# Three heads' columns of a weight block, loaded two rows to a partition by loads of eight partitions

## The chip, the cores and the metric

The kernel runs on one core of a Trainium2 chip. The metric is the device time of one execution in microseconds (us). The core has a matrix engine (TensorE, PE in the profile; its weight loads are PEld), a vector engine (VectorE, DVE), a scalar engine (ScalarE, ACT), GpSimd (POOL) and SyncE (SP), which here only issues transfers (DMAs). The transfers run on 16 DMA engines. On-chip memory (SBUF) has 128 partitions; matmuls write to banks of PSUM, each 128 partitions by 512 float32.

## The reference

A decode step of one transformer block: two batch rows of one token, D = 512, 32 query heads of 128, 8 key/value heads, a window of the last 4096 cached positions, a feed-forward layer of 1792. All is float32.

```python
mod = (silu(c) @ w_mod).reshape(2, 6, 1, -1)          # sa, ca, ga, sb, cb, gb
h = layernorm(x) * (1 + ca) + sa
q = h @ wq                                            # wq: 512 x 4096
# k, v: the last 4096 of 32768 positions, 8 heads, each used by 4 query heads
o = softmax(q k^T * 128**-0.5) v
x = x + ga * (o @ wo)                                 # wo: 4096 x 512
h = layernorm(x) * (1 + cb) + sb
x = x + gb * (silu(h @ w1) @ w2)                      # w1: 512 x 1792, w2: 1792 x 512
```

Keys and values are 64 MiB of the 97.5 MB that are read; the weights are the rest. Every weight, key and value is read once.

## The kernel before

**The stream.** All large operands pass through one ring of eight buffers of [128, 4096] float32 (`stream`, L69, `RING = 8`). A buffer can be filled again when everything that read it is done, so the transfer into the n-th buffer taken waits for the last reader of the (n-8)-th. All transfers are issued by SP, one after the other, in this order: `wm0` (the first 128 rows of `w_mod`, L103), four small ones for `c` and `x` (`c_ch`, `x_ch`, L107: four partitions each), `wm1` to `wm3` (L111), `wq0` to `wq3` (L112), then `fetch(0)` and `fetch(h + 1)` in the head loop: two tiles of keys (L79) and, from the second head on, two of values (L86) for each key/value head; at the end four tiles of `wo` (L473), a small one for `x` again (`x_sp`, L474), three of `w1` and five of `w2` (L95). The transfers' completions are counted on eight semaphores, taken in turn, so a ninth transfer isn't issued before the first of its eight has landed.

**The start.** `c` is put through silu and multiplied with `w_mod` in four steps of 128 rows (L241 to L255); layernorm of `x` runs beside it. The modulated row is transposed to `hq_T` (L263): [128, 4, 32], where `hq_T[p, k, :]` belongs to row 128*k + p of `wq`; of its 32 columns two hold the batch rows.

**The query projection** (L280 to L291). For each of the four row blocks k and each half n of the heads, four matmuls, one for each g = 0 to 3, write to partitions 32g to 32g+31 of the PSUM bank `q_ps[n]`. Head number 16n + 4s + g has its 128 columns at place s of that row group, so one matmul covers four heads, s = 0 to 3, 512 columns. The 16 matmuls of a row block wait for its tile of `wq`. Behind it (L292 to L311) q is transposed and spread into `qbd`, which the first scores need.

**The head loop** (L447 to L467). For each of the eight key/value heads VectorE transposes the keys (L337, eight instructions a head), TensorE forms scores (L349), and softmax, the turned probabilities and the product with the values (L423) follow one head later. In the loop the program's order is kept on each engine (`inorder`).

**The end.** `o @ wo` (L548 to L567), the second layernorm, `w1` (L593), silu, `w2` (L628 to L651; the last tile holds one row of `w2` a partition, 2 KB), the last two VectorE instructions (L653, L654) and the transfer of the output (L656). `busy` puts matmuls without use between (`junk`).

Of the kernel before, what the change touches and what calls it, by code (L numbers as in the profile page):

```python
# [13 lines left out]
P = 128  # L14
B, D = 2, 512
HQ, HKV, DH = 32, 8, 128
# [7 lines left out]
def adaln_block(  # L24
# [21 lines left out]
    nc = tc.nc  # L46
# [16 lines left out]
    def const(shape, name):  # L63
        return consts.tile(shape, F32, name=name)

    def bank(tag, name):
        return (psum1 if tag in "CO" else psum).tile([P, 512], F32, tag=tag, name=name)

    def stream(name):  # L69
        return ring.tile([P, 4096], F32, tag="st", name=name)  # L70

    def load_rows(name, w, k, width):
        t = stream(f"{name}{k}")[:, :width]
        nc.sync.dma_start(t, w[k * P : (k + 1) * P, :])
        return t
# [33 lines left out]
                src[b, :].rearrange("(k a c) -> a k c", k=4, a=4),  # L109
            )  # L110
    wm += [load_rows("wm", w_mod, k, 6 * D) for k in range(1, 4)]  # L111
    wqt = [load_rows("wq", wq, k, HQ * DH) for k in range(4)]  # L112


    ident = const([P, P], "ident")
# [125 lines left out]
    for k in range(4):  # L241
        ab = wm[k][:, : 2 * D].rearrange("p (s k a c) -> p a s k c", s=2, k=4, a=4)
        cd = wm[k][:, 2 * D :].rearrange("p (s g m) -> p g s m", s=4, g=4)
        for g in range(4):
            r = slice(32 * g, 32 * g + 32)
            nc.tensor.matmul(m_ch[r, :], scT[:, k, :], ab[:, g], start=(k == 0), stop=(k == 3))
        for g in range(4):
            r = slice(32 * g, 32 * g + 32)
# [13 lines left out]
    hq_T = const([P, 4, 32], "hq_T")  # L262
# [13 lines left out]
    nc.gpsimd.memset(uT, 0.0)  # L276

    q_ps = [bank("D", f"q{n}") for n in range(2)]  # L280
    for k in range(4):
        wv = wqt[k].rearrange("p (n s g m) -> p n g s m", n=2, s=4, g=G)
        for n in range(2):
            for g in range(G):
                nc.tensor.matmul(  # L285
                    q_ps[n][32 * g : 32 * g + 32, :],
                    hq_T[:, k, :],
                    wv[:, n, g],
                    start=(k == 0),
                    stop=(k == 3),  # L290
                )  # L291
    for n in range(2):  # L292
        qT = once.tile([P, D], F32, tag="wide", name=f"qT{n}").rearrange("p (s j r) -> p s j r", s=4, r=32)
        nc.vector.transpose(qT.rearrange("p s j r -> p (s j r)"), q_ps[n])  # L294
        for g in range(G):
            r = slice(32 * g, 32 * g + 32)
            eng = nc.gpsimd if g % 2 else nc.vector
            eng.tensor_copy(
                qg[n][r, :, :, :, g], qT[r, :, :, 0:32:16].rearrange("p s j b -> p s b j")
            )  # L300
        rp = bank("C", f"qr{n}")[:, :P]
        nc.tensor.matmul(
            rp, rep4, qg[n].rearrange("p s b j g -> p (s b j g)"), start=True, stop=True
        )
        for i in range(4):
            r = slice(32 * i, 32 * i + 32)
            cp = nc.scalar.copy if i % 2 else nc.vector.tensor_copy
            cp(
                qbd[n][r].rearrange("p s b j c -> p (s b j) c")[:, :, 4 * i : 4 * i + 4],
                rp[r, :].rearrange("p (m g) -> p m g", g=G),  # L310
            )  # L311
# [183 lines left out]
    for r in (0, 64):  # L495
# [4 lines left out]
            start=True,  # L500
            stop=True,
# [46 lines left out]
    for q in range(24):  # L548
        g = q % 4
# [4 lines left out]
            start=(q < 4),  # L554
            stop=(q >= 20),
# [3 lines left out]
    for q in range(24, 32):  # L559
        for g in range(4):  # L560
# [4 lines left out]
                start=(q == 24),  # L565
                stop=(q == 31),
# [26 lines left out]
    for k in range(4):  # L593
        for g in range(4):
# [4 lines left out]
                start=(k == 0),  # L599
                stop=(k == 3),  # L600
# [28 lines left out]
    for tt in range(WIDE):  # L629
        g = tt % 4  # L630
# [4 lines left out]
            start=(tt < 4),  # L635
            stop=(tt >= WIDE - 4),
# [4 lines left out]
    for tt in range(WIDE, T2):  # L641
        for g in range(4):
# [4 lines left out]
                start=(tt == WIDE),  # L647
                stop=(tt == T2 - 1),
# [35 lines left out]
```

## Time and profile before

| | us |
|---|---|
| median of 3 runs (237.0 to 237.11) | 237.1 |
| the profiled execution, as timed | 236.89 |
| its span, first to last instruction | 235.0 |
| busy: PE / DVE / ACT / POOL | 146.5 / 114.6 / 25.4 / 10.3 |
| time of the packets of the DMA queue that carries the data, share of 16 engines' span | 97.5% |
| bytes read | 97.53 MB, 415 GB/s over the span |

A profile line for an instruction group gives the source line, the engine, the operation, output<-input, the shapes and the count. The chain is followed back from the last instruction, at each step to what released it. "DMA wq" in it means that the chain ran through the landing of a transfer of `wq`. Besides the instructions the trace holds a record of each DMA packet: start, bytes and duration, not the engine that carried it. A row of 16 KB is one packet; each of the DMA engines that takes part in a transfer ends its share with one packet of 4 bytes.

### The profile page before, as it was taken

How to read it: one execution, taken by the hardware profiler on the slowest of the kernel's cores; microseconds unless marked ns; L12 is line 12 of the kernel's file. 1: busy time of each engine (PE TensorE's matmuls, PEld its weight loads, DVE VectorE, ACT ScalarE, POOL GpSimd, SP SyncE). 2: the span in 40 equal slices, each digit the busy share in tenths (PEclk: the TensorE clock that was granted, in tenths of full speed). 3: DMA queues.
4: the chain of work that ended last, by engine and by line, in shares of the span. 5: the costliest groups of instructions: out<-in, count | busy, mean ns of one | idle time of the engine just before them, and what ended most of it. 6: DMA issues, size and time to landing. Idle time of an engine off the chain costs nothing.

```text
span 235.0 us, 2644 instructions
## 1 busy us (share of the span) xinstructions
PE 146.5 (62%) x1094; PEld 45.9 (20%) x1094; DVE 114.6 (49%) x176; ACT 25.4 (11%) x56; POOL 10.3 (4%) x30
## 2 busy tenths in 40 slices
PE   0086546367187577667549519626743967788993
PEld 0032101101011121121112102111211222335332
DVE  0634000793694792693892792595298050002130
ACT  2200000100300200200200200200020021003210
POOL 8600000100000000000000000000000000000000
PEclk9999975759869997999976967965985799999999
DMA  6999999999999999999999999999999999999991
GB/s 253 426 438 427 427 438 427 424 439 427 429 441 424 427 438 427 429 438 424 429 435 429 427 432 432 432 429 432 428 429 429 429 432 429 432 426 422 421 412 56
DMA packets 7603, 97.69 MB, mean 416 GB/s; under 512 B 920, under 2 KB 936, under 8 KB 1576
## 3 DMA queue, kind: packets, MB, share of 16 engines
q1 hardware_dynamic: 7592, 97.54, 97.5%
q8 instruction: 8, 0.13, 0.2%
q14 instruction: 3, 0.02, 0.0%
HBM read 97.53 MB, written 0.00 MB: 415 GB/s over the span
## 4 chain that ended last, share of the span: by engine, by line
DMA 64%; DVE 22%; PE 10%; ACT 2%; issue 1%; SPq 1%; DVEq 0%
DVE kT L337 16%; DMA wo<-in_A_wo_dram 14%; DMA k<-in_A_k_cache_dram 14%; DMA v<-in_A_v_cache_dram 13%; DMA wq<-in_A_wq_dram 13%; DMA w<-in_B_w_dram 7%; PE s L349 5%; DMA wm<-in_w_mod_dram 3%; DVE zp L395 2%; PE o L423 2%; PE q L285 1%; DVE xp L393 1%; ACT pr L381 1%; DVE mx L359 1%; ACT L381 1%
## 5 line engine op out<-in xcount | busy, mean ns | idle before, releaser
L337 DVE STREAM_TRANSPOSE kT<-k 128x1024 f32<-128x1024 f32 x64 | 73.7, 1210 | 1.6 <-DMA k<-in_A_k_cache_dram 1.6
L349 PE MATMUL s<-kT,qbd 128*32 128x512 f32 x256 | 44.5, 670 | 11.2 <-DVE kT L337 11.1
L423 PE MATMUL o<-v,ptb 128*32 128x512 f32 x256 | 38.5, 730 | 19.8 <-DMA v<-in_A_v_cache_dram 19.3
L359 DVE TENSOR_REDUCE mx<-s 128x1 f32<-128x512 f32 x8 | 5.5, 691 | 40.1 <-PE s L349 40.1
L349 PEld LDWEIGHTS s<-kT,qbd 128*32 128x32 f32 x256 | 11.1, 126 | 45.8 <-issue 24.1
L285 PE MATMUL q<-wq,hq_T 128*32 128x512 f32 x64 | 11.2, 836 | 10.1 <-DMA wq<-in_A_wq_dram 10.1
L423 PEld LDWEIGHTS o<-v,ptb 128*32 128x32 f32 x256 | 8.1, 124 | 35.8 <-issue 33.1
L402 PE MATMUL pT<-zp,id 128*32 128x256 f32 x64 | 5.6, 418 | 13.9 <-DVE zp L395 13.9
L379 ACT COPY bias<-bp 128x1 f32<-128x1 f32 x8 | 1.3, 159 | 111.9 <-PE bp L377 111.9
L537 PE MATMUL junk<-selh,id 128*32 128x256 f32 x46 | 11.3, 380 | 0.0
L294 DVE STREAM_TRANSPOSE qT<-q 128x512 f32<-128x512 f32 x2 | 1.4, 718 | 18.6 <-PE q L285 18.3
L395 DVE TENSOR_TENSOR zp<-xp,group 128x1024 f32<-128x1024 f32 x8 | 9.8, 1225 | 0.2
L393 DVE STREAM_TRANSPOSE xp<-pr 128x512 f32<-128x512 f32 x8 | 5.6, 701 | 4.4 <-ACT pr L381 4.4
L217 PE MATMUL mean_a<-mv_a,avg 128*128 128x1 f32 x2 | 0.6, 362 | 10.6 <-DVE mv_a L214 10.6
L361 PE MATMUL mT<-ident,mx 128*1 128x128 f32 x16 | 3.0, 270 | 6.4 <-DVE mx L359 6.4
L550 PE MATMUL acc_o<-wo,oTn 128*32 128x512 f32 x48 | 5.8, 598 | 1.9 <-DMA wo<-in_A_wo_dram 1.6
L537 PEld LDWEIGHTS junk<-selh,id 128*32 128x32 f32 x46 | 5.0, 110 | 6.7 <-issue 3.5
L438 PE MATMUL o_all<-ob,selh 128*64 128x128 f32 x64 | 5.7, 304 | 0.8 <-ACT ob L432 0.8
L270 DVE STREAM_TRANSPOSE xT<-x_sp 128x128 f32<-128x128 f32 x1 | 0.4, 403 | 11.8 <-DMA x_sp<-in_A_x_dram 11.8
L432 ACT COPY ob<-o 128x512 f32<-128x512 f32 x8 | 4.7, 585 | 10.3 <-PE o L423 10.3
L285 PEld LDWEIGHTS q<-wq,hq_T 128*32 128x32 f32 x64 | 2.1, 128 | 18.8 <-DMA wq<-in_A_wq_dram 12.5
L249 PE MATMUL m_sp<-wm,scT 128*32 128x512 f32 x32 | 5.7, 796 | 0.0
(132 smaller groups left out, 95.0 us busy)
## 6 DMA issues: line engine op xcount, KB each, us to landing
k<-in_A_k_cache_dram SPq DMA_DIRECT2D x16, 2048.0 KB, 30.2
v<-in_A_v_cache_dram SPq DMA_DIRECT2D x16, 2048.0 KB, 31.5
wq<-in_A_wq_dram SPq DMA_DIRECT2D x4, 2048.0 KB
wo<-in_A_wo_dram SPq DMA_DIRECT2D x4, 2048.0 KB, 32.3
wm<-in_w_mod_dram SPq DMA_DIRECT2D x4, 1536.0 KB, 10.2
w<-in_B_w_dram SPq DMA_DIRECT2D x2, 1024.0 KB, 23.2
w<-in_B_w_dram SPq DMA_DIRECT2D x1, 1792.0 KB
w<-in_B_w_dram SPq DMA_DIRECT2D x2, 896.0 KB
```

Source lines behind the costliest of these rows:

```text
L249: nc.tensor.matmul(m_sp[r, :], scT[:, k, :], cd[:, g], start=(k == 0), stop=(k == 3))
L285: nc.tensor.matmul(q_ps[n][32 * g : 32 * g + 32, :], hq_T[:, k, :], wv[:, n, g], start=(k == 0), stop=(k == 3),)
L337: inorder(nc.vector.transpose(kT[h, b][:, :, 8 * n4 : 8 * n4 + 8, :].rearrange("p j n k -> p n j k"), kt[h, b][:, n4 * 1024 : (n4 + 1) * 1 ...
L349: inorder(nc.tensor.matmul(s_ps[h][r : r + 32, :], qbd[h // 4][:, h % 4, b, j, :], kT[h, b][:, j, 16 * c : 16 * c + 16, :], start=(j == 0) ...
L359: inorder(nc.vector.tensor_reduce(mx, s_ps[h], axis=AX.X, op=ALU.max))
L393: inorder(nc.vector.transpose(xp, pr[h]))
L395: inorder(nc.vector.tensor_mul(zp, xp[:, None, :, 0:16].to_broadcast([P, 4, 16, 16]), group[:, :, None, None].to_broadcast([P, 4, 16, 16]),))
L402: inorder(nc.tensor.matmul(tp[32 * i : 32 * i + 32, :], id4, zp.rearrange("p a s x -> p (a s) x")[:, :, 4 * i : 4 * i + 4], start=True, st ...
L423: inorder(nc.tensor.matmul(o_ps[h][32 * c : 32 * c + 32, :], ptb[h % 2][:, 256 * b + 32 * w : 256 * b + 32 * w + 32], vt[h, b][:, 512 * w ...
L438: inorder(nc.tensor.matmul(o_all[r : r + 64, :], selh[:, m, HQ - G - G * h : 3 * HQ - G - G * h], o_sb[h][:, m * DH : (m + 1) * DH], start ...
L537: inorder(nc.tensor.matmul(junk[0:32, :256], id4, selh.rearrange("p m y -> p (m y)")[:, :256], start=True, stop=True,))
L550: inorder(nc.tensor.matmul(acc[32 * g : 32 * g + 32, :], oTn[:, q, :], wot[q // 8][:, q % 8, :], start=(q < 4), stop=(q >= 20),))
```

## The change

The total of bytes stays the same. Rows 384 to 511 of `wq` (the fourth block) were loaded as 128 partitions of 4096 columns. Now that load covers columns 0 to 3711, and columns 3712 to 4095 (heads 29, 30 and 31) go to another buffer of the ring, `wqx`, two rows to a partition: partition p of 0 to 63 holds rows 384 + 2p and 384 + 2p + 1. Eight loads fill it. Each covers eight partitions, p0, p0+4, ..., p0+28, for p0 = 0, 1, 2, 3, 32, 33, 34, 35, and so 16 pieces of 1536 bytes. They are issued in pairs behind `wq0`, `wq1`, `wq2` and `wq3`. `wqx` is taken from the ring before `wq0`.

The left factor for these rows has to be laid out likewise: two matmuls with every second column of the identity pick `hq_T[2p + j, 3, :]` into a PSUM bank, and one VectorE copy moves it to `hx` ([64, 2, 32]). In the fourth block of the projection, the matmuls of n = 1 and g = 1, 2, 3 stop at 384 columns, and for each of these two matmuls over 64 partitions (j = 0, 1) and 128 columns add the fourth head.

```diff
-    wqt = [load_rows("wq", wq, k, HQ * DH) for k in range(4)]
+    WX = 3 * DH
+    WN = HQ * DH - WX
+    wqt, wqx = [], stream("wqx")[:, : 2 * WX].rearrange("p (j e) -> p j e", j=2)
+    rows2 = wq[3 * P :, WN:].rearrange("(p j) e -> p j e", j=2)
+    for k in range(4):
+        if k < 3:
+            wqt.append(load_rows("wq", wq, k, HQ * DH))
+        else:
+            wqt.append(stream("wq3"))
+            nc.sync.dma_start(wqt[3][:, :WN], wq[3 * P :, :WN])
+        for p0 in ((0, 1), (2, 3), (32, 33), (34, 35))[k]:
+            nc.sync.dma_start(wqx[p0 : p0 + 29 : 4], rows2[p0 : p0 + 29 : 4])
...
+    hx = const([P // 2, 2, 32], "hx")
+    hxp = bank("B", "hxp")[: P // 2, :64]
+    for j in range(2):
+        nc.tensor.matmul(
+            hxp[:, 32 * j : 32 * j + 32], ident[:, j:P:2], hq_T[:, 3, :], start=True, stop=True
+        )
+    nc.vector.tensor_copy(hx.rearrange("p j c -> p (j c)"), hxp)
...
             for g in range(G):
+                r = slice(32 * g, 32 * g + 32)
+                part = k == 3 and n == 1 and g > 0
+                s1 = 3 if part else 4
                 nc.tensor.matmul(
-                    q_ps[n][32 * g : 32 * g + 32, :],
+                    q_ps[n][r, : s1 * DH],
                     hq_T[:, k, :],
-                    wv[:, n, g],
+                    wv[:, n, g, :s1, :],
                     start=(k == 0),
                     stop=(k == 3),
+                    skip_group_check=True,
                 )
+                for j in range(2 if part else 0):
+                    nc.tensor.matmul(
+                        q_ps[n][r, 3 * DH :],
+                        hx[:, j, :],
+                        wqx[: P // 2, j, (g - 1) * DH : g * DH],
+                        start=False,
+                        stop=(j == 1),
+                        skip_group_check=True,
+                    )
```

## The prediction

> **What bounds the kernel now.** I read the slices and the queues first, then the chain, then the stages, then SP's waits. The slices and queues of the page:
>
> ```profile
> DMA  6999999999999999999999999999999999999991
> ...
> q1 hardware_dynamic: 7592, 97.54, 97.5%
> q8 instruction: 8, 0.13, 0.2%
> q14 instruction: 3, 0.02, 0.0%
> ```
>
> From the second slice to the last but one the 16 DMA engines are at 90% or more; PE is busy for 62% of the span, DVE for 49%. Eight packets of 16 KB (q8) and three of 8 KB (q14) fetch instructions. The stages and the end of the chain:
>
> ```profile
> 23.00:46.00 23.00, 12.19 (x68) 2.63 (x68) 3.31 (x11) 0.82 (x4) 0.94 (x4) 0.76 1.01 432
> 46.00:90.00 44.00, 27.07 (x154) 6.37 (x158) 33.26 (x34) 4.70 (x11) 0.00 (x0) 0.85 1.01 431
> ```
>
> ```profile
> 39.01 3.39 PE q L285 x16
> ...
> 213.97 16.51 DMA w<-in_B_w_dram
> 230.48 0.04 issue
> 230.53 1.10 PE acc_y L643 x24
> 231.63 0.02 issue
> 231.66 0.30 DVE yo L653
> 231.96 0.02 issue
> 231.98 0.29 DVE yo L654
> ```
>
> The stage with the changed projection (23 to 46 us) has a DMA share of 1.01: the queue never runs dry. So the chain's 3.39 us of q after the last tile of `wq` is no price of the whole; the end comes from the landing of the last `w2` tiles, plus a tail of some 4 us that the change doesn't touch. What counts is when the **slowest of the 16 engines** has moved its share.
>
> That is in the trace's packet records (zero of the span is 10.5 us on their clock, from matching landings). In the full stream an engine's packets follow one another with a fixed step: 607 ns for 16 KB, 532 for 14 KB, 80 for 2 KB, 23.5 for 512 bytes, 6 for a closing 4-byte packet. Following each packet to the one that starts where it ended gives 16 unbroken chains from 24 us to the end. Their only breaks are instruction fetches: each 16 KB fetch delays one chain, by 0.9 us and mostly another 0.5 some 1.1 us later; each 8 KB fetch delays one by 0.3 and up to 0.5. The eight 16 KB fetches hit eight different chains. The last closing packets, in us of the span:
> - five chains without a fetch: 229.05, 229.33, 229.45, 229.48, 229.60
> - three with an 8 KB fetch: 229.87, 229.99, 230.35
> - eight with a 16 KB fetch: 230.52, 230.72, 230.94, 231.01, 231.05, 231.06, 231.10, 231.13
>
> The spread of 2.08 us at the end is what a shift of bytes between engines can win or lose.
>
> **Which engines the change loads.** The `c_ch` and `x_ch` loads have four partitions each; their 64 packets of 128 bytes sit on four chains. The `x_sp` load's eight packets also sit on four, and these end at 229.33, 229.45, 229.99 and 230.35: all in the early half, where four of 16 drawn at random would lie in 70 of 1820 cases. So I take it that a load of eight partitions goes to eight engines, these four among them, and that the eight are the early half. The second step is a choice: nothing in the trace names the other four. The Trainium skill (DMA: Bandwidth & Descriptors, Why a DMA increments its semaphore by 16 and not by 1) says that the engine count is the largest up to 16 that divides the outermost sizes, on the lowest-numbered engines; the four chains of the four-partition loads agree.
>
> **The cost of each part.**
> - *The shortened load.* Every engine had eight packets of 16384 bytes for `wq3`; now they have 14848. Between 532 ns (14336) and 607 (16384) that is 551: 8 x 56.4 ns = **0.45 us less on all 16**.
> - *The eight small loads.* 16 packets of 1536 bytes on each of eight engines. Between 23.5 ns (512) and 80 (2048) one takes 61.2: 16 x 61.2 = 0.98, and eight closing packets of 6 ns, 0.05. **1.03 us more on eight engines, net +0.58.** Beyond the packets a small load may leave a gap. Lower bound 0: the `x_sp` load in the full stream took its engines two steps of 23.5 and a 6, and the 14 KB packets behind it kept their 532. Upper bound: behind the four small loads at the start, the first 12 KB packets of the four engines took 519, 582, 594 and 632 ns instead of 460, so up to 0.17 us; once for each of the four pairs that is 0.69. I take 0: `x_sp` stands in a full stream as these will, the others in the first 7 us.
> - The Trainium skill (the same page, Bandwidth) has 0.68 us for 4 KB and 0.95 for 64 KB and calls transfers under 64 KB descriptor-dominated; interpolated for 24 KB, eight in series would be an estimated 6 us, and the kernel slower by that. The `x_sp` row, 0.05 us on its engines, says that such a time is latency and passes beneath the stream.
> - *SP.* Eight more issues at 0.52 to 0.72 us (the `c_ch`, `x_ch` issues) are 5 us of SP between 7 and 28 us. At most eight transfers are out: `wq0` waits for `wm0`'s landing, the 1.8 us here:
>
> ```profile
> SPq L74 <- DMA wm<-in_w_mod_dram: 1.8, 1, 1.8
> ```
>
> With eight more in the row, the second loads behind `wq1`, `wq2` and `wq3` wait for `wm1`, `wq0` and `wq1`. Each time at least two 2 MB tiles, 9.8 us, stay queued. `wqx` moves the ring by one: `wq3` waits for `wm0`'s readers (16.1 us), and the fourth key tile for `wqx`'s, the last matmuls of q, at about 43 us, with three key tiles still out, due 4.9 us apart behind `wq3`'s 39: by 44, 49 and 54 us. Behind it on SP stand two value and two key tiles, all due after 58 us. No engine starves: 0. If the last q matmul came 10 us later, it would. From then on the ring pairs the same tiles as before, and eight is a whole turn of the semaphores.
> - *PE, DVE.* Two picking matmuls (qr's took 319 ns each) and a copy (about 0.2 us) fall at 22 to 23 us, where PE waits for `wq`. Behind `wq3`, three matmuls lose a quarter and six of 128 columns come (278 ns each on `acc_y`), with six more weight loads of 128 ns: 0.3 to 1.0 us later q, and so qT, qbd and the first kT transposes. VectorE needs 4.6 us for a tile that takes 4.9 to load, and key transfers are issued 30.2 us ahead of their landing (median), so 0; without that cover, 1.0.
> - *Instruction fetches.* The 16 KB fetches came when 100, 228, 368, 472, 620, 712, 861 and 998 matmuls had started, about one in 128; a ninth would come near 1126. The change makes 1094 into 1102: still eight. SP's new instructions may move an 8 KB one.
>
> **The sum.** The late eight: 231.13 - 0.45 = 230.68. The early eight: their last, 230.35 + 0.58 = 230.93, is now the end. 231.13 to 230.93 is **-0.2 us**: span 234.8, the profiled execution 236.7 (236.89 - 0.2), and from the median of 237.1 (0.2 above the profiled execution) **236.9**.
>
> **The rivals.**
> 1. *Full gain.* The early chain of 230.35 gets its 8 KB fetch elsewhere or starts sooner (the five untouched ones differ by 0.55 us), and the late half decides: -0.45, and with the spread of starts 0.35 to 0.6: 236.65. For: it is a single chain that holds the end; the next stand at 229.99 + 0.58 = 230.57. Against: its fetch at 47 us may come again.
> 2. *The eight engines aren't the early half.* Some of the late, fetch-hit chains are among them: 231.13 + 0.58, +0.58 us: 237.7 at the worst, 237.3 if the one of 230.72 is the latest of them (231.30, +0.17). For: only four of the eight are located. It decides as soon as a late chain ending above 230.55 is among them.
> 3. *Gaps behind the small loads.* Each pair costs its engines 0.17 us: 230.93 + 0.69 = 231.62, +0.49: 237.6. For: the 582 to 632 ns packets above. Against: `x_sp`. Slower than before from 0.2 us in all, 50 ns a pair.
> 4. *The change doesn't shift.* The small loads spread over all 16: 8 x 61.2 + 48 - 451 = +0.09 on each, 237.2. The Trainium skill (the same page, Rules for kernel authors) says that transfers to disjoint halves of the partitions both spray over all 16 engines, which would give this; the four chains of the four-partition loads speak against it, and no run here has a half-partition load.
>
> **Chances.** Forecast 0.40, full gain 0.28, wrong half 0.14, gaps 0.10, no shift 0.08. Range: the forecast and the full gain down to 236.5, rivals 2 to 4 up to 237.7; a ninth fetch (+0.9 on a late engine, 237.5) lies inside. The likeliest alone: 236.75 to 237.05. About 0.2%, 0.47 us, is what a measurement of this kernel can tell from no change. The full gain is about half beyond it (0.14), and 0.06 is for timed runs whose late chains stand out more than the profiled one's: faster 0.2. Rivals 2 and 3 pass it mostly, and a ninth fetch would: slower 0.22. Same 0.58.
>
> **What would show it.** In the profile after: DMA share still full between 23 and 46 us; packets of 1536 bytes on eight chains; `wq3`'s packets of 14848 bytes; the spread of the last closing packets about 1.3 us instead of 2.1, with an `x_sp` chain among the last; the last `w2` landing 0.2 to 0.45 us earlier; q later by 0.3 to 1 us without an effect on the end. I am wrong if the last landing moves by more than 0.5 us, if the queue runs dry near 54 us, or if steps behind the small packets exceed those of the size.

## The result and the profile after

The changed kernel takes 238.05 us (median of 7 runs, 237.87 to 239.23) against 237.1 before (7 runs, 237.0 to 237.29): 1.0047 times as long, 95% interval 1.0035 to 1.006. That is 0.95 us more; the forecast was 0.2 us less, and 238.05 lies above the range. The profiled execution has a span of 235.9 us (235.0 before). Five more runs among the experiments gave 238.38 (ratio 1.0053, 1.004 to 1.0065).

The slices and queues of the changed kernel's page:

```profile
DMA  6999999999999999999999999999999999999991
GB/s 250 427 422 425 411 422 434 436 418 433 439 425 422 445 428 422 439 433 417 436 439 420 428 445 428 418 442 433 414 439 439 417 431 445 425 421 426 420 405 50
...
q1 hardware_dynamic: 7784, 97.54, 97.3%
q8 instruction: 9, 0.15, 0.2%
q14 instruction: 3, 0.02, 0.0%
```

The DMA engines are as full as before and move the same 97.54 MB. The ninth 16 KB instruction fetch comes at 232.4 us, behind the last load, and costs nothing. The end of the chain of waits:

```profile
214.80 16.52 DMA w<-in_B_w_dram
231.33 0.04 issue
231.37 1.09 PE acc_y L678 x24
232.46 0.02 issue
232.49 0.30 DVE yo L688
232.79 0.02 issue
232.81 0.29 DVE yo L689
```

The last `w2` tiles land 0.84 us later (PE starts at 231.37, 230.53 before); the tail behind them is the same. So the loss is in the stream. It is found by stages of 10 us; the columns are the stage, its length, the busy time of PE, PEld, DVE, ACT and POOL (in brackets the number of instructions), the granted clock, the DMA share and the rate in GB/s. First the kernel before, then the changed one:

```profile
12.00:22.00 10.00, 8.11 (x66) 2.77 (x66) 3.33 (x11) 0.85 (x2) 0.28 (x1) 1.00 1.02 435
22.00:32.00 10.00, 5.12 (x32) 1.02 (x32) 0.74 (x4) 0.00 (x0) 0.25 (x1) 0.83 1.01 431
32.00:42.00 10.00, 5.78 (x32) 1.05 (x32) 0.94 (x3) 0.00 (x0) 0.12 (x1) 0.66 1.01 431
42.00:52.00 10.00, 4.57 (x12) 0.95 (x8) 8.37 (x14) 1.03 (x4) 0.82 (x4) 0.67 1.00 427
52.00:212.00 160.00, 104.64 (x745) 31.32 (x745) 91.89 (x105) 16.99 (x42) 0.00 (x0) 0.86 1.01 430
```

```profile
12.00:22.00 10.00, 8.60 (x66) 2.92 (x66) 2.84 (x9) 0.73 (x2) 0.00 (x0) 1.00 1.02 436
22.00:32.00 10.00, 4.79 (x32) 1.32 (x36) 1.33 (x6) 0.12 (x1) 0.53 (x1) 0.86 1.01 411
32.00:42.00 10.00, 6.05 (x37) 1.06 (x30) 1.10 (x3) 0.00 (x0) 0.47 (x2) 0.84 1.00 424
42.00:52.00 10.00, 4.89 (x21) 2.12 (x20) 5.07 (x10) 1.03 (x4) 0.47 (x2) 0.84 1.02 437
52.00:212.00 160.00, 110.67 (x744) 31.14 (x743) 95.04 (x108) 16.44 (x41) 0.00 (x0) 0.87 1.01 430
```

From 22 to 32 us, where the small loads behind `wq0` and `wq1` pass, the stream moves 411 GB/s and not 431, **at the same DMA share of 1.01**. The queue isn't empty; packets take longer. 20 of 431 GB/s over 10 us is 0.46 us, as a mean over the 16 engines. Before that stage the rates agree, and from 32 to 52 us they do on average (424 and 437 against 431 and 427).

The packet records say which. The 128 pieces of 1536 bytes sit on eight chains, 16 on each. One piece in a full stream takes 65 ns. Behind `wq0` they took 102 ns on average and up to 324, behind `wq1` 149 and up to 361, behind `wq2` and `wq3` each of the 64 took 65. A pair of loads held its engine 0.26 us where undisturbed, as forecast, 0.40 on average behind `wq0` and 0.66 behind `wq1`; the tiles `wq1` and `wq2` behind them were slowed too. In sum an engine of the eight lost 0.82 us on average (0.15 + 0.40 in the pairs, 0.05 + 0.22 in the tiles).

The last closing packets, on the scale of the prediction:

| engines | before | after |
|---|---|---|
| the eight with small loads | not told apart | 230.09, 231.00, 231.11, 231.18, 231.78, 231.81, 231.93, 231.94 |
| the other eight | not told apart | 229.28, 229.37, 230.64, 230.76, 230.77, 230.80, 230.81, 230.81 |
| latest of all | 231.13 | 231.94 |

The engine isn't in the record, and chains that run at the same phase can be taken for one another; but the four latest are of the eight. Two of these (231.78 and 231.94) also carry a 16 KB instruction fetch; six of the other eight do.

### The profile page after: what moved, and what is told of

It is laid out like the page before. It is cut to its first block, busy times and chain, and to the rows that moved or that the text cites. A ratio compares the mean times of both kernels' runs of the same rounds, so it can differ in the third digit from the quotient of the medians.

```text
span 235.9 us, 2689 instructions
## 1 busy us (share of the span) xinstructions
PE 154.1 (65%) x1110; PEld 47.7 (20%) x1110; DVE 114.6 (49%) x177; ACT 25.4 (11%) x56; POOL 10.3 (4%) x30
## 3 DMA queue, kind: packets, MB, share of 16 engines
q1 hardware_dynamic: 7784, 97.54, 97.3%
## 4 chain that ended last, share of the span: by engine, by line
DMA 49%; DVE 31%; PE 15%; ACT 3%; issue 1%; SPq 0%; DVEq 0%
DVE kT L372 23%; DMA wo<-in_A_wo_dram 14%; DMA wq<-in_A_wq_dram 13%; DMA k<-in_A_k_cache_dram 12%; PE s L384 9%; DMA w<-in_B_w_dram 7%; DVE zp L430 3%; DMA wm<-in_w_mod_dram 3%; PE q L310 2%; DVE xp L428 2%; ACT pr L416 2%; DVE mx L394 1%; PE q L319 1%; PE mT L396 1%; PE bp L412 1%
## 5 line engine op out<-in xcount | busy, mean ns | idle before, releaser
L384 PE MATMUL s<-kT,qbd 128*32 128x512 f32 x256 | 50.5, 699 | 13.3 <-DVE kT L372 13.3
L458 PE MATMUL o<-v,ptb 128*32 128x512 f32 x256 | 37.1, 707 | 12.0 <-DMA v<-in_A_v_cache_dram 11.5
L384 PEld LDWEIGHTS s<-kT,qbd 128*32 128x32 f32 x256 | 11.7, 129 | 52.8 <-DVE kT L372 28.0
L310 PE MATMUL q<-wq,hq_T 128*32 128x512 f32 (+1 forms) x64 | 12.0, 737 | 8.8 <-DMA wq<-in_A_wq_dram 8.8
L412 PE MATMUL bp<-negscale,mrow 1*128 1x1 f32 x16 | 3.0, 256 | 4.2 <-DVE mrow L405 4.2
## 6 DMA issues: line engine op xcount, KB each, us to landing
wo<-in_A_wo_dram SPq DMA_DIRECT2D x4, 2048.0 KB, 32.2
```

The source lines that it names most:

```text
L310: nc.tensor.matmul(q_ps[n][r, : s1 * DH], hq_T[:, k, :], wv[:, n, g, :s1, :], start=(k == 0), stop=(k == 3), skip_group_check=True,)
L384: inorder(nc.tensor.matmul(s_ps[h][r : r + 32, :], qbd[h // 4][:, h % 4, b, j, :], kT[h, b][:, j, 16 * c : 16 * c + 16, :], start=(j == 0) ...
L458: inorder(nc.tensor.matmul(o_ps[h][32 * c : 32 * c + 32, :], ptb[h % 2][:, 256 * b + 32 * w : 256 * b + 32 * w + 32], vt[h, b][:, 512 * w ...
```

## The experiments

Each ran beside the kernel before on the same chip; ratios are to that. The theories' letters are explained where they first stand in the expectations.

**The place and the rows.** In the first run, four small loads each behind `wq2` and `wq3`:

```diff
-        for p0 in ((0, 1), (2, 3), (32, 33), (34, 35))[k]:
+        for p0 in ((), (), (0, 1, 2, 3), (32, 33, 34, 35))[k]:
```

> The eight small loads as in the change, but four behind wq2 and four behind wq3, none behind wq0 and wq1. Theory G (gaps: in the changed kernel the small loads behind wq0 and wq1 held their eight engines 0.3 to 0.85 us a pair where 0.26 was due, those behind wq2 and wq3 exactly 0.26): if the gaps belong to the early place, they are gone, 0.8 us comes back, 237.1 to 237.3 us, and every group of small loads takes 0.26 us a pair. If they belong to whichever small loads come first, they appear behind wq2 and the time stays near 238. Theory S (shares: eight engines have 0.58 us more to move and some of them were late already) and theory C (the query projection ends 3.1 us later) both expect 238.0, unchanged.

Measured: 239.39 us (237.84 to 240.76), ratio 1.0088 (1.0054 to 1.0122). The early place isn't needed: the pieces behind `wq2` took 162 ns on average, 31 of the 64 over 90; those behind `wq3` 65. Here as in the change the gaps come with the loads that pass first. A second loss is new: from 36 to 42 us 16 KB packets took up to 2.1 us on some engines, when the slow pieces were past and the later ones took 65 ns. Its cause isn't settled. The stage of that run:

```profile
32.00:42.00 10.00, 7.53 (x43) 1.67 (x36) 1.38 (x4) 0.16 (x1) 0.47 (x2) 0.71 0.99 359
```

In the second the two halves change places, `((32, 33), (34, 35), (0, 1), (2, 3))[k]`.

> The eight small loads as in the change, with the pairs in the other order: partitions 32 to 63 (rows 448 to 511) behind wq0 and wq1, partitions 0 to 31 (rows 384 to 447) behind wq2 and wq3. G: if the gaps come from the rows that are read, they move to the pairs behind wq2 and wq3; if from the place in the stream, they stay behind wq0 and wq1. The time stays near 238.0 in both, and by S and C too: this run is read from the packets.

Measured: 238.17 (237.92 to 238.41), ratio 1.0042 (1.0029 to 1.0054). The gaps stayed behind `wq0` and `wq1` (109 and 161 ns a piece; 65 behind `wq2` and `wq3`). It isn't these rows.

**Equal shares.** Four loads of 16 partitions, on all 16 engines:

```diff
-        for p0 in ((0, 1), (2, 3), (32, 33), (34, 35))[k]:
-            nc.sync.dma_start(wqx[p0 : p0 + 29 : 4], rows2[p0 : p0 + 29 : 4])
+        for p0 in (k,):
+            nc.sync.dma_start(wqx[p0 : p0 + 61 : 4], rows2[p0 : p0 + 61 : 4])
```

> The same buffer, the same pieces of 1536 bytes and the same matmuls, but four loads of 16 partitions (p0, p0+4, ..., p0+60), one behind each tile of wq, so that all 16 engines have the same share (+0.05 us each). S: 237.1 to 237.2 us, as before. C: 238.0, since the projection is the same. G: half as many pieces on an engine at a time; gaps at the first two loads would leave 237.3 to 237.6.

Measured: 238.89 (238.18 to 239.44), ratio 1.0073 (1.0058 to 1.0088). By S this should have been the time before. But the run doesn't decide on S, since another loss came in: the pieces were hardly slow (65 to 77 ns on average), but the whole stream fell to a slower pace:

```profile
32.00:42.00 10.00, 7.33 (x41) 1.10 (x33) 0.72 (x1) 0.00 (x0) 0.00 (x0) 0.62 1.01 400
42.00:52.00 10.00, 4.88 (x22) 2.07 (x22) 5.75 (x12) 1.03 (x4) 0.95 (x4) 0.89 1.00 391
52.00:212.00 160.00, 106.32 (x733) 30.62 (x735) 94.82 (x108) 16.45 (x41) 0.00 (x0) 0.83 1.01 430
```

From 40 to 49.5 us every 16 KB packet on every engine took 675 to 688 ns instead of 611. Just after an 8 KB instruction fetch at 50.0 us all were back at 611; an earlier slow stretch of this run ended near 30 us, with no fetch at that moment (the nearest came at 27.9 us).

**The shares alone, in whole rows**, with the projection of before:

```diff
-    wqt = [load_rows("wq", wq, k, HQ * DH) for k in range(4)]
+    wqt = [load_rows("wq", wq, k, HQ * DH) for k in range(3)]
+    wqt.append(stream("wq3"))
+    nc.sync.dma_start(wqt[3][:112], wq[3 * P : 3 * P + 112, :])
+    for p0 in (112, 120):
+        nc.sync.dma_start(wqt[3][p0 : p0 + 8], wq[3 * P + p0 : 3 * P + p0 + 8, :])
```

> The kernel before, with its projection unchanged; only the load of the fourth block of wq is split: 112 partitions in one load (seven 16 KB rows an engine) and the last 16 in two loads of eight partitions. All engines lose one packet of 607 ns, eight get two: +0.61 us on eight engines, -0.61 on the other eight, all in whole 16 KB rows. G: no small pieces, no gaps; if the eight engines were the early half, -0.2 us, 236.9. S: some of the eight were late, the end moves by up to +0.6: 237.5 to 237.7. C: 237.1.

Measured: 243.32 (242.87 to 243.65), ratio 1.0258 (1.0245 to 1.0271), ten times any theory's price. The experiment changed more than shares:

```profile
22.00:32.00 10.00, 5.47 (x32) 1.09 (x32) 0.00 (x0) 0.00 (x0) 0.00 (x0) 0.83 1.02 436
32.00:42.00 10.00, 3.62 (x16) 0.62 (x16) 0.00 (x0) 0.00 (x0) 0.00 (x0) 0.74 1.09 233
42.00:52.00 10.00, 5.13 (x20) 1.69 (x20) 2.97 (x9) 0.70 (x3) 0.95 (x4) 0.50 0.92 369
```

From 32.2 to 36.3 us, where by the order of issue the 112-partition load passes, most 16 KB packets took 0.85 to 1.02 us. Behind it pass the two eight-partition loads, which cover neighbouring partitions here: the 16 packets from 38.6 to 40.6 us took 2.35 to 2.47 us, four times 611 ns. The records don't say which load a packet is of, so it isn't shown that only those two loads were slow, or why. The Trainium skill (SBUF — State Buffer, Door 1: The DMA port swizzle) has four neighbouring partitions on one of 16 ports; a factor of four agrees with it. As a test of S the run says nothing.

**Where the pieces lie.** The small loads stay as in the change, on the same engines, partitions and places in the stream; only their source changes. First rows of `w1`, 7 KB apart, so that neighbouring engines' pieces stand 56 KB apart and not 128:

```diff
-    rows2 = wq[3 * P :, WN:].rearrange("(p j) e -> p j e", j=2)
+    rows2 = w1[:P, :WX].rearrange("(p j) e -> p j e", j=2)
```

> The changed kernel with one difference: the eight small loads take their 128 pieces of 1536 bytes from the first 384 columns of 128 rows of w1 instead of wq's. The rows stand 7 KB apart there, so that the pieces that eight engines read together stand 56 KB apart and not 128 KB. (Heads 29 to 31 get wrong values for the last 128 rows of the projection.) Theory A (the pieces collide in memory because they stand a power of two apart): no gaps, every pair of small loads takes 0.26 us, the stream loses under 0.15 us, 237.1 to 237.3. Theory Q (any small load in a full stream leaves gaps early on, wherever its bytes stand): gaps as in the change, 238.0.

Measured: 237.29 (236.85 to 237.35), ratio 1.0009 (1.0 to 1.0017). The loss is gone, with the shares of the change: unequal shares (S) aren't what costs the 0.95 us. Three of the four groups took 65 ns a piece, one 66.

A compact stretch of `w2`, pieces 1792 bytes apart, those of neighbouring engines 14 KB:

```diff
+    rows2 = w2[:112, :].rearrange("r e -> (r e)").rearrange("(p j e) -> p j e", j=2, e=448)[:, :, :WX]
```

> As the run before it, but the pieces come from one compact stretch of 229 KB of w2, 1792 bytes apart, the pieces of eight engines 14 KB apart. A: no gaps, 237.1 to 237.3; if the collision is of another kind than one of powers of two (pieces close together share what they collide on), gaps as large or larger, 238 or more. Q: 238.0.

Measured: 237.25 (236.87 to 237.52), ratio 1.0007 (0.9998 to 1.0015); all 128 pieces 65 ns. The stage that had 411 GB/s in the change, in these two runs, `w1` first:

```profile
22.00:32.00 10.00, 6.27 (x32) 1.10 (x32) 0.04 (x1) 0.00 (x0) 0.00 (x0) 0.73 1.01 430
```

```profile
22.00:32.00 10.00, 5.63 (x32) 1.10 (x32) 0.20 (x2) 0.00 (x0) 0.00 (x0) 0.58 1.01 426
```

The same stretch for the loads of 16 partitions (with the same wrong values in heads 29 to 31):

> The four loads of 16 partitions (the run with equal shares, 238.89 us) with the pieces from the compact stretch of w2. In that run all 16 engines took 675 to 684 ns for a 16 KB packet instead of 611, from 24 to 30 us and from 32 to 50 us. A: that came from the collision of the pieces and is gone, 237.1 to 237.3. Theory P (engines 8 to 15 write into partitions 32 to 63, which other engines fill, and the stream then stays in a slower state): 238.5 or more again. Q: some loss, 237.5 to 238.5.

Measured: 239.15 (237.42 to 240.57), ratio 1.0088 (1.0054 to 1.0121). The profiled execution was the fastest, 237.42, and still lost 0.4 us (237.02 before), with all engines' 16 KB packets 70 ns longer from 29 to 32 us. So the slower pace came with pieces 14 KB apart too. P is left, with its reason untested: what differs from the run before is that 16 engines and not eight fill partitions 0 to 63.

**The later projection**, in the kernel before:

```diff
+    slow = bank("B", "slow")
...
         for n in range(2):
+            for _ in range(4 if k == 3 and n == 1 else 0):
+                nc.tensor.matmul(slow[0:32, :], hq_T[:, k, :], wv[:, n, 0], start=True, stop=True)
```

> The kernel before, with four matmuls without use of 512 columns, one after the other, ahead of the second half of the fourth block of the projection, so that q ends about 3 us later as in the changed kernel; all loads as before. Theory C (the later q costs): +0.9 us, 238.0. If the stream alone sets the end: 237.1, with the DMA queue full throughout.

Measured: 237.0 (236.82 to 237.35), ratio 1.0004 (0.9995 to 1.0013). The stream hides it; C falls.

**Which property of the place.** Other memory, the same distance: a part of the key cache that isn't read otherwise, as rows of 16 KB.

```diff
+    rows2 = k_cache.rearrange("b h s d -> (b h s d)")[: P * 4096].rearrange("(p j e) -> p j e", j=2, e=4096)[:, :, WN:]
```

> The changed kernel, but the pieces come from a stretch of the key cache that nothing else reads, seen as 128 rows of 16 KB, the last 1536 bytes of each: the same 128 KB between the pieces of neighbouring engines as in wq, in other memory. (Heads 29 to 31 get wrong values for the last 128 rows of the projection, here and in the next run.) Theory A (the pieces collide with each other because of their distance): gaps as in the change, 237.9 to 238.3. Theory D (they collide with the rows of wq that stream beside them, or it is wq's place in memory): no gaps, 237.1 to 237.3.

Measured: 237.96 (237.74 to 238.32), ratio 1.0036 (1.0024 to 1.0049). The loss is back, so the pieces needn't come from `wq`. But it came at another place: the pieces behind `wq0`, `wq1` and `wq2` took 65 ns, those behind `wq3` 188 on average. The same memory with rows 1536 bytes longer, 140 KB between engines (`P * 4480`, `e=4480`):

> As the run before it, but the rows are 16 KB + 1536 bytes apart, so that neighbouring engines' pieces stand 140 KB apart and no two at the same place of a 128 KB step. A: no gaps, 237.1 to 237.3. If scattered pieces in that memory are slow in themselves, 238 as in the run before it. D: 237.1 to 237.3.

Measured: 237.24 (237.13 to 237.38), ratio 1.0005 (0.9996 to 1.0014); all 128 pieces 65 ns. The stage with the last two pairs in both runs, 128 KB first:

```profile
32.00:42.00 10.00, 8.15 (x46) 1.81 (x38) 1.10 (x3) 0.00 (x0) 0.47 (x2) 0.70 1.01 410
```

```profile
32.00:42.00 10.00, 6.17 (x42) 1.52 (x37) 1.10 (x3) 0.00 (x0) 0.47 (x2) 0.93 1.00 424
```

The small loads' place in the stream, engines, sizes and memory are the same in these two. Only the row pitch differs: 128 or 140 KB between neighbouring engines, 16 or 17.5 KB between the two pieces of a partition. **How far apart the pieces stand decides whether this stream loses 0.8 us.**

With what they collide isn't shown. Theory A says with one another. But in the run with 128 KB the pieces of the first three groups stood as far apart as those of the fourth, and took 65 ns. They passed beside rows of `wq`; the fourth passed beside the first rows of the keys, which lie in the same key cache, and those rows, too, took up to 0.87 us instead of 611 ns. In the change it is the other way round: slow beside rows of `wq`, 65 ns beside the keys. This fits a wider form of theory D, that the pieces collide with rows of the same tensor that stream beside them, when the distances are such. `w1` and `w2` don't stream yet when the small loads pass, so the two runs with their rows can't tell A from this; it wasn't tested by itself.

The change once more in the same set:

> The changed kernel once more, as the measure for the two before it on the same chip: 237.9 to 238.5 by every theory; its spread from run to run (237.87 to 239.23 before) shows how much the gaps vary.

Measured: 238.38 (237.95 to 238.73), ratio 1.0053 (1.004 to 1.0065); gaps behind `wq0` and `wq1`, 107 and 119 ns a piece.

**A mending.** The rows dealt out so that neighbouring engines read neighbouring rows, 16 KB apart:

```diff
-    rows2 = wq[3 * P :, WN:].rearrange("(p j) e -> p j e", j=2)
+    rows2 = wq[3 * P :, WN:].rearrange("(l j i) e -> l i j e", l=8, j=2)
...
-            nc.sync.dma_start(wqx[p0 : p0 + 29 : 4], rows2[p0 : p0 + 29 : 4])
+            nc.sync.dma_start(wqx[p0 : p0 + 29 : 4], rows2[p0 // 32 * 4 + p0 % 32])
```

> The changed kernel with the rows dealt out otherwise, its computation whole: the load number l of eight partitions takes rows 384 + 16l + i and 384 + 16l + 8 + i for its partitions i = 0 to 7, so that neighbouring engines read rows 16 KB apart and not 128 KB; one more VectorE copy lays the columns of the identity out for it. Theory A, if only the steps of 128 KB collide: no gaps, 237.2 to 237.3, the same as with the pieces from other memory. A, if any power of two of 16 KB or more collides: 237.9 to 238.5, as the change. By either it isn't faster than before, since two of the eight engines that get the 0.58 us also carry a 16 KB instruction fetch: the end comes 0 to 0.1 us later than before without any gap.

Measured: 237.97 (237.66 to 238.3), ratio 1.0038 (1.0024 to 1.0052), gaps behind `wq1` (123 ns a piece). Steps of 16 KB between the engines don't help. They weren't tried alone: the two pieces of a partition stand 128 KB apart in this run. Rows of `wq` are always a multiple of 16 KB apart; distances of an odd number of rows above one weren't tried.

## Why the prediction was wrong

*What bounds the kernel* held: the DMA share, the slowest engine's last landing and an unchanged tail of 4 us. *SP*, the ring and the semaphores held: the queue didn't run dry near 54 us, and the second loads behind `wq1` to `wq3` waited where it said. *Eight engines* for loads of eight partitions held: 16 pieces on each of eight chains, and 64 closing packets more than before, eight a load.

**The step that failed** is "Beyond the packets a small load may leave a gap ... I take 0: `x_sp` stands in a full stream as these will". The eight engines lost 0.82 us each on average, more than the upper bound of 0.69 taken from the first packets behind `c_ch` and `x_ch`. This is the third rival's place and sign, with a price of 0.95 us in the runs and not 0.49; its mechanism is another. The load that was compared with, `x_sp`, reads one stretch of 4 KB; the change's pieces stand 128 KB apart. What the source addresses do was no term of the sum, and no row of before showed it. With pieces 56, 14 or 140 KB apart, in other tensors, the gaps were gone and the time was 0.05 to 0.09% above the kernel before.

**A second step was wrong**, and would have cost the gain without gaps: that the eight engines are the early half. In the run with 140 KB the two latest chains are of the eight, carry a 16 KB fetch and end at 231.10 and 231.28 (231.13 the latest before); the other eight end by 230.85. So 0.58 us more on eight engines and 0.45 less on the others came out 0.15 us later in that profile and 0.12 in the median (237.24 against 237.12), not 0.2 earlier. That is the second rival, in part. The choice rested on four located engines; the four others were assumed.

*Sizes.* An undisturbed pair took 0.256 us (0.257 by the steps of the sum), eight packets of 14848 bytes with their closing one 4.41 us (8 x 551 ns): right. The later q was mis-sized: forecast 0.3 to 1.0 us, measured 3.1. The instructions of the fourth block in the changed kernel (start, busy, engine; weight loads and other engines left out; the 12 of the first line are ten of 512 and two of 384 columns):

```profile
38.84 3.04 PE L310 MATMUL q<-wq,hq_T 128*32 128x512 f32 x12 [2.68 <-DMA wq<-in_A_wq_dram]
...
41.81 1.06 PE L319 MATMUL q<-wqx,hx 64*32 64x128 f32 x4
...
42.80 0.86 PE L310 MATMUL q<-wq,hq_T 128*32 128x384 f32 x2
...
43.58 0.62 PE L319 MATMUL q<-wqx,hx 64*32 64x128 f32 x4
...
44.13 0.83 PE L310 MATMUL q<-wq,hq_T 128*32 128x384 f32 x2
...
44.90 0.62 PE L319 MATMUL q<-wqx,hx 64*32 64x128 f32 x4
```

A matmul of the program stands as two instructions in the trace: the 16 of a row block before are eight matmuls, and the six short ones, which the forecast counted as six, are twelve. Before, 16 took 3.39 us at a granted clock of 0.57; here 28 take 6.7 at 0.74. So the clock has a part in the 3.1 us. At a clock of 1.00, in the run with 140 KB, the 28 took 5.08 us and the 16 of the block ahead of them 1.92: before, the instructions of the four row groups start within 0.03 us of one another, while those of the groups with three matmuls mostly start one behind the other. The later q cost nothing, as forecast: the run with four added matmuls, in which q ended 3.3 us later, took 237.0. *Instruction fetches*: by the same count the eight new matmuls make 1094 into 1110 and not 1102, and a ninth 16 KB fetch did come, behind the last load.

What stays open: with what the pieces collide, and why some pairs beside rows of `wq` are free: the one behind `wq2` in the change, and nearly all pieces behind `wq0` and `wq2` in the run with 16 KB. The packets allow a reading: in the change the 32 pieces of the first pair start within 0.6 us of one another, those of the third, after the collisions, within 1.4. Engines that were thrown out of step would then be safe. That wasn't tried by itself, and being in step isn't enough for a collision: with the key cache the pieces of the first three pairs start within 0.43 us and are free. Open too are the slower pace with 16 engines and the second loss of the first experiment.

## What to carry to other kernels

When loads are cut up to even out the engines, look at the distance between the bytes that the engines read at the same moment: pieces of 1.5 KB at steps of 16 or 128 KB cost more than the evening-out could bring, and pieces of the same size 14, 56 or 140 KB apart, read from other tensors, left no gaps. Look also at what streams beside them: with loads of eight partitions, the slow groups all passed beside rows of their own tensor. Before bytes are moved between engines, every late engine has to be located in the trace, not a likely half. And a DMA share of 1.0 doesn't show that the stream runs at its rate: read the GB/s of the stage beside it.

## What the runs showed of the hardware

- Short pieces 128 KB apart from engine to engine took up to 361 ns instead of 65 in the changed kernel, and up to 333 with 16 KB from engine to engine, though not in every group: with the key cache three groups of four at 128 KB took 65. The Trainium skill (DMA: Bandwidth & Descriptors, Latency and other measured facts) tells of copies within memory that slow down at row pitches of 2 MB and more, full again when a pitch of 4 MB is made 4 KB longer, and infers, without having verified it, that streams in lockstep meet on the same channel. The runs here agree in kind (all groups at 140 KB were free, one of four at 128 KB wasn't), for loads to on-chip memory and at steps far smaller than its own; which part of the memory is shared they don't show.
- While two loads of eight neighbouring partitions passed, 16 KB packets took 2.35 to 2.47 us instead of 0.61; in the changed kernel a pair of loads of eight partitions four apart, in pieces of 1.5 KB, held its engines 0.26 us where nothing collided.
- A full stream stayed slow by a tenth for 10 us without a visible cause, at 681 ns a packet of 16 KB instead of 611 and a DMA share of 1.00.
